# The first stretch of a fused attention and mixture kernel, in an order planned inside the kernel

## The chip, the cores and the metric

The kernel runs on one core of a Trainium2 chip. The metric is the device time of one execution in microseconds. Three runs of the kernel before took 1064.70, 1065.81 and 1065.82 us; the median is 1065.81.

## The reference

Three layers follow each other. The input is 4 batches of 8 heads, 576 tokens and 64 columns a head.

```python
# 1 attention, causal by blocks of 64 tokens
scores = q @ k.T / 8;  scores = where(block_i >= block_j, scores, -1e9)
attn = exp(scores - max) / (sum + 1e-9);  x = attn @ v     # heads side by side: (2304, 512)
# 2 dense unit: maximum of three products, then w_out
h = maximum(maximum(x @ w1, x @ w2), x @ w3)               # 512 -> 768
x = h @ w_out                                              # 768 -> 512
# 3 eight experts (512 -> 1024 -> 512), two per token
noisy = x @ w_gate + log1p(exp(x @ w_noise)) * noise       # the top two, softmax over them
out = sum over the two: weight * (maximum(x @ w1[e], 0) @ w2[e])
```

The weights of the dense layer arrive as 64-bit floats, all else in 32 bits.

## The kernel before

**Attention in jobs.** A job is two heads (a pair) of one batch. Early jobs cover the first 256 tokens of a batch in plain fp32, late jobs the other 320 with each operand split into a high and a low half and three products in place of one. `JOBS` lists them: four early jobs of batch 0, four of batch 1 (jobs 0 to 7), then `MIDDLE`, late and early jobs mixed. Jobs 0 to 7 share four sets of buffers (`SETS`), three of which lie in the tiles that late jobs use afterwards, so that late work can begin only when those jobs are through. An early job has these steps: scores on TensorE (`s_early`, L268), maxima and their scaling on DVE (L275, L277), exponentials on ACT (L280), sums and reciprocals on DVE (L285, L286), scaling of the exponentials on ACT (L294), six turns by TensorE with copies by DVE (`t_early`, L326, L327), and the products with the values (`pv_early`, L360, L361), whose result goes to SBUF as input of a dense unit (L365 for batch 0).

**Dense units.** Nine units of 256 tokens pass layer 2. Unit u < 8 belongs to batch u // 2, even units to early jobs. Unit 0 is computed in plain fp32 from the widened weights (`hidden0`, L519; `columns0`, L541), as the weights are not yet split then; all others with split weights (`hidden`, L561 to L563). The chain `fill` yields them step by step, and `filler(budget)` draws steps of a given cost into the gaps between the steps of the jobs. `CH` is their order, and a unit may be drawn only when its jobs are through (`ready`).

**Weights.** The 64-bit weights come in 24 pieces of 512 KB (18 of the three matrices, six of `w_out`) through 12 staging places. `widen` makes fp32 of a piece: two integer steps on DVE (L438, L439), the low bits on ACT (L440), an integer addition on GpSimd (POOL, L444), and then the load of the piece 12 further on (L432). The gate weights are multiplied into `w_out` (`load_gates`: 24 turns, L456, and 48 small products, L464), so that the columns of unit 0 come in a product of 512 and one of 16. `part` splits the weights into halves (ACT L500, POOL L501): six parts a matrix, then `w_out`. The halves take the places of staging tiles and of widened matrices, and so wait for the additions or products that read those.

**What sets the order.** The program emits steps with generators: `weights(n)` draws n steps of widening, gates or splitting in each gap, `WS` of them, and `warm` issues products of ones (L87), whose results are not used, to keep TensorE busy: 14 ahead of the jobs and three in each gap of jobs 0 to 3. `need(flag)` draws weight steps until a stage is done. All is then ordered by the framework's scheduler, which takes for each engine the ready instruction that was emitted first, by times of its own. Each engine's queue, and SP's queue of loads, runs in the order that results.

Of the kernel before, what the change touches and what calls it, by code (L numbers as in the profile page):

```python
# [36 lines left out]
CH = (0, 2, 4, 1, 6, 3, 5, 7)  # L37
# [15 lines left out]
PER = (0.0, 2.0, 1.0, 1.2)  # L53
WS = (2, 4)
WARM = 3
# [9 lines left out]
def tile_attention_moe_moe(ctx, tc, qT, kT, v, w1, w2, w3, w_out, gates, noise, e1, e2, out):  # L65
# [201 lines left out]
    def s_early(j, c, blocks):  # L267
        st = new_stats(j)  # L268
        q, k, _, p, _ = SET[SETS[j] if j < 8 else 0]
        ps = bank("s")  # L270
        o = (0, 256)
        for x, i in zip(o, blocks):
            nc.tensor.matmul(ps[:, x:x + 64 * i + 64], q[:, i], k[:, :64 * i + 64], start=True, stop=True)
        for a, (x, i) in enumerate(zip(o, blocks)):
            nc.vector.tensor_reduce(st[:, 0, c + a:c + a + 1], ps[:, x:x + 64 * i + 64], axis=AX.X, op=OP.max,  # L275
                                    negate=True)
        nc.vector.tensor_scalar(st[:, 0, c:c + 2], st[:, 0, c:c + 2], 0.125, None, op0=OP.mult)  # L277
        for a, (x, i) in enumerate(zip(o, blocks)):
            n = 64 * i + 64
            nc.scalar.activation(p[:, POFF[i]:POFF[i] + n], ps[:, x:x + n], AF.Exp, bias=st[:, 0, c + a:c + a + 1],  # L280
                                 scale=0.125, accum_out=st[:, 1, c + a:c + a + 1])

    def scale(j, c0, blocks):
        st = ST[j][:, 1, c0:c0 + len(blocks)]
        nc.vector.tensor_scalar(st, st, 1.0e-9, None, op0=OP.add)  # L285
        nc.vector.reciprocal(st, st)  # L286
        for c, i in enumerate(blocks):
            s = ST[j][:, 1, c0 + c:c0 + c + 1]
            if i > 3:
                P = PL[i][:, :64 * i + 64]  # L290
                nc.vector.tensor_scalar(P, P, s, None, op0=OP.mult)
            else:
                P = SET[SETS[j] if j < 8 else 0][3][:, POFF[i]:POFF[i] + 64 * i + 64]
                nc.scalar.activation(P, P, AF.Copy, scale=s)  # L294

# [23 lines left out]
    def t_early(j, key):  # L319
        p, pt = SET[SETS[j] if j < 8 else 0][3:]  # L320
        ps = bank("t")
        blocks = range(4) if key == 0 else (2, 3)
        n = len(blocks)
        for a, i in enumerate(blocks):
            o = POFF[i] + 128 * key
            nc.tensor.transpose(ps[:, 128 * a:128 * a + 128], p[:, o:o + 128], ident)  # L326
        nc.vector.tensor_copy(pt[:, :, 256 * key:256 * key + 64 * n].rearrange("p h (i c) -> p h i c", c=64),  # L327
                              ps[:, :128 * n].rearrange("p (i h c) -> p h i c", i=n, h=2))
# [4 lines left out]
    def new_x(u, g):  # L333
        if u == 8:
            while "u0" not in given:
                next(fill)
            need("so")
            return keep.tile([128, 2, D], F32R, name="xs")
# [13 lines left out]
    EP = {}  # L352

    def pv_early(j, r):
        late, b, g = JOBS[j]
        V, _, pt = SET[SETS[j] if j < 8 else 0][2:]
        if r == 0:
            EP[j] = bank("t")[:, :256]
        p, m = EP[j], slice(64 * r, 64 * r + 64)
        nc.tensor.matmul(p[m], V[:, r, 0:64], pt[:, r, 0:256], start=True, stop=False)  # L360
        nc.tensor.matmul(p[m, 128:256], V[:, r, 64:128], pt[:, r, 256:384], start=False, stop=True)  # L361
        if r:
            x = new_x(2 * b, g)
            if b == 0:
                nc.scalar.activation(x, p, AF.Copy)  # L365
            else:
                nc.scalar.activation(x[:, 0], p, AF.Copy)
                nc.vector.tensor_sub(x[:, 1], p, plain(x[:, 0]))
# [43 lines left out]
    shifted = psS.tile([128, 2, 512], I32, name="a2")  # L412
# [14 lines left out]
    def load_piece(n):  # L427
        if n >= 24:
            return
        src, dst = piece(n)  # L430
# [3 lines left out]
    def widen(n):  # L434
        r, t = stage[n % NW // 3][:, n % 3], shifted[:, n % 2]
        dst = piece(n)[1].bitcast(I32)
        hi, lo = r[:, :, 1], r[:, :, 0]
        nc.vector.tensor_scalar(t, hi, 3, 0x3FFFFFFF, op0=OP.logical_shift_left, op1=OP.bitwise_and)  # L438
        nc.vector.scalar_tensor_tensor(hi, hi, -0x40000000, t, op0=OP.bitwise_and, op1=OP.bitwise_or)  # L439
        nc.scalar.activation(lo, r.bitcast(U16).rearrange("p c (t h) -> p c t h", h=2)[:, :, 0, 1], AF.Copy,  # L440
                             scale=2.0 ** -13)
# [3 lines left out]
        load_piece(n + NW)  # L445

    def load_gates():
        gt = PL[5][:, 128:192].rearrange("p (k n) -> p k n", k=4)
        nc.sync.dma_start(gt, gates.rearrange("(k p) n -> p k n", p=128))
        for g in range(3):  # L450
            wt = []
            for c in range(2):
                ps = bank()
                for k in range(4):
                    o = 256 * c + 128 * (k // 2)
                    nc.tensor.transpose(ps[:, 128 * k:128 * k + 128], WPO[2 * g + k % 2][:, o:o + 128], ident)  # L456
                t = PL[7 + c][:, :512]
                nc.scalar.activation(t, ps, AF.Copy)
                wt += [t[:, 0:256], t[:, 256:512]]
                yield  # L460
            ps = bank()
            for j in range(2):
                for k in range(4):
                    nc.tensor.matmul(ps[:, 2 * E * j:2 * E * j + 2 * E], wt[k][:, 128 * j:128 * j + 128], gt[:, k],  # L464
                                     start=k == 0, stop=k == 3)
            nc.vector.tensor_copy(WPG[:, 2 * g:2 * g + 2], ps[:, :4 * E].rearrange("p (f n) -> p f n", f=2))
            yield

    given = set()

    def convert():
        for n in range(24):
            widen(n)
            if n % 6 == 5:
                given.add(n // 6)
            yield
        for _ in load_gates():
            yield
        given.add("g")

    conversion = convert()
    todo = []

    def weights(n):
        for _ in range(n):
            if next(conversion, 0) == 0 and todo:
                todo.pop(0)()
# [7 lines left out]
    def part(n, i, j, src, flag=None):  # L495
        def do():
            while "g" not in given:
                weights(1)
            wh, wl = (w[:, i, j] for w in halves(n))
            nc.scalar.activation(wh, src, AF.Copy)  # L500
            nc.gpsimd.tensor_sub(wl, src, plain(wh))  # L501
            if flag is not None:
                given.add(flag)
        todo.append(do)

    def need(flag):
        while flag not in given:
            weights(1)

    def hidden0(parts):  # L510
        for fp in range(3):
            need(fp)
            m = None
            for n in ("1", "2", "3"):
                ps = bank().rearrange("p (a b) -> p a b", a=2)
                for j in range(2):
                    f = (2 * fp + j) * 128
                    for kt in range(4):
                        nc.tensor.matmul(ps[:, j], WP[n][:, kt, f:f + 128], XT[0, kt],  # L519
                                         start=kt == 0, stop=kt == 3)  # L520
                if m is None:
                    m = moe.tile([128, 2, UT], F32, name="hh", bufs=3)
                    nc.scalar.activation(m, ps, AF.Copy)
                else:
                    nc.vector.tensor_max(m, ps, m)
                yield 3.3
            parts.append(m)
        for n in ("1", "2", "3"):
            for fp in range(3):
                for k in (0, 2):  # L530
                    s = slice(k, k + 2), slice(256 * fp, 256 * fp + 256)
                    part(n, *s, WP[n][:, s[0], s[1]], ("s", n, fp) if k else None)

    def columns0(parts, tt, x2, gl):
        for w, n in ((WPO, DM), (None, 2 * E)):
            if w is None:
                need("g")
                w = [WPG[:, ft] for ft in range(6)]
            ps = bank()
            for ft in range(6):  # L540
                nc.tensor.matmul(ps[:, :n], parts[ft // 2][:, ft % 2, tt * 128:tt * 128 + 128], w[ft],  # L541
                                 start=ft == 0, stop=ft == 5)
            if n == DM:
                nc.scalar.activation(x2, ps, AF.Copy)
            else:
                nc.vector.tensor_copy(gl[:, tt], ps[:, :n])
            yield n / 100.0

    def hidden(u, parts):
        steps = 0  # L550
        for fp in range(3):
            m = None
            for n in ("1", "2", "3"):
                need(("s", n, fp))
# [46 lines left out]
    def moe1(u):  # L601
        parts = []
        yield from hidden(u, parts) if u else hidden0(parts)
        done.add(u)
        yield 0.01
        need("so" if u else 3)
# [602 lines left out]
```

## Time and profile before

| | |
|---|---|
| Profiled execution | 1064.64 us, span 1062.8 us |
| Mean granted TensorE clock | 0.972 of full speed |
| TensorE busy | 1011.0 us, 95% |
| DVE, ACT, POOL busy | 489.6, 420.2, 457.2 us |
| Moved by DMA | 107.31 MB, mean 101 GB/s |

TensorE is abbreviated PE. Starts and stretches are counted from the start of the span. Matmuls overlap, so that the sum of their durations is more than the time that they take; the spacing of their starts tells that. An fp32 product counts as two matmuls in the rows. The page's chain of waits ends after one step in this case and is of no use; waits and timeline take its place.

### The profile page before, as it was taken

How to read it: one execution, taken by the hardware profiler on the slowest of the kernel's cores; microseconds unless marked ns; L12 is line 12 of the kernel's file. 1: busy time of each engine (PE TensorE's matmuls, PEld its weight loads, DVE VectorE, ACT ScalarE, POOL GpSimd, SP SyncE). 2: the span in 40 equal slices, each digit the busy share in tenths (PEclk: the TensorE clock that was granted, in tenths of full speed). 3: DMA queues.
4: the chain of work that ended last, by engine and by line, in shares of the span. 5: the costliest groups of instructions: out<-in, count | busy, mean ns of one | idle time of the engine just before them, and what ended most of it. 6: DMA issues, size and time to landing. Idle time of an engine off the chain costs nothing. (4 is left out here: it accounts for less than half of the span.)

```text
span 1062.8 us, 17401 instructions
## 1 busy us (share of the span) xinstructions
PE 1011.0 (95%) x6591; PEld 909.2 (86%) x6591; DVE 489.6 (46%) x1324; ACT 420.2 (40%) x1001; POOL 457.2 (43%) x381
## 2 busy tenths in 40 slices
PE   8379999999999999899899899999999999999997
PEld 4257778999999999899899888879898988989895
DVE  6932267596668883885525432122222213222221
ACT  5652344565545662665312333324132323232110
POOL 4750334133232423232314358776564747565302
PEclk9678999999999999999899999999999999999999
DMA  9911032241112120211301256554353534443101
GB/s 292 272 67 26 12 129 73 80 131 41 49 34 70 48 71 16 70 48 46 95 21 51 62 161 219 162 182 155 118 182 93 179 117 131 148 137 120 55 14 64
DMA packets 76263, 107.31 MB, mean 101 GB/s; under 512 B 23672, under 2 KB 48248, under 8 KB 76176
## 3 DMA queue, kind: packets, MB, share of 16 engines
q1 hardware_dynamic: 65584, 76.76, 23.8%
q0 software_dynamic: 10592, 29.41, 8.5%
q8 instruction: 53, 0.87, 0.3%
q14 instruction: 34, 0.28, 0.1%
HBM read 86.66 MB, written 20.53 MB: 101 GB/s over the span
## 5 line engine op out<-in xcount | busy, mean ns | idle before, releaser
L129 POOL TENSOR_TENSOR w<-rw,w 128x1536 fp32r<-128x1536 f32 (+1 forms) x45 | 141.2, 3140 | 76.0 <-ACT w L128 64.3
L128 ACT ACTIVATE w<-rw 128x1536 fp32r<-128x1536 f32 (+1 forms) x45 | 60.4, 1343 | 108.8 <-DMA rw<-in_e 56.7
L939 PE MATMUL b<-xh,w 128*128 128x384 f32 (+7 forms) x272 | 87.0, 321 | 0.9 <-ACT xh L929 0.9
L940 PE MATMUL b<-xl,w 128*128 128x384 f32 (+7 forms) x272 | 87.2, 320 | 0.1
L941 PE MATMUL b<-xh,w 128*128 128x384 f32 (+7 forms) x272 | 87.1, 320 | 0.0
L561 PE MATMUL t<-xA,w 128*128 128x256 f32 x288 | 82.4, 286 | 1.1 <-DVE hm L568 0.9
L562 PE MATMUL t<-xB,w 128*128 128x256 f32 x288 | 82.4, 287 | 0.0
L561 PE MATMUL t<-xB,w 128*128 128x256 f32 x288 | 82.3, 287 | 0.0
L563 PE MATMUL t<-xB,w 128*128 128x256 f32 x288 | 82.0, 285 | 0.0
L562 PE MATMUL t<-xA,w 128*128 128x256 f32 x288 | 81.8, 284 | 0.0
L563 PE MATMUL t<-xA,w 128*128 128x256 f32 x288 | 81.5, 283 | 0.0
L988 POOL DMA_INDIRECT out_rows<-y,isc x40 | 40.5, 1012 | 79.7 <-DVE y L987 72.7
L576 POOL TENSOR_TENSOR hl<-hm,hh 128x512 fp32r<-128x512 f32 x21 | 27.3, 1299 | 107.7 <-ACT hh L575 88.7
L944 DVE SCALAR_TENSOR_TENSOR ht<-b,ht 128x384 fp32r<-128x384 f32 (+6 forms) x56 | 29.1, 520 | 95.8 <-ACT ht L943 95.8
L220 POOL TENSOR_TENSOR Kl<-rk,Kh 128x576 fp32r<-128x576 f32 x16 | 23.7, 1479 | 114.7 <-ACT Kh L219 72.1
L983 PE MATMUL b<-w,ht 128*128 128x512 f32 (+1 forms) x168 | 67.3, 401 | 3.6 <-ACT ht L943 3.6
L941 PE MATMUL t<-xh,w 128*128 128x256 f32 x240 | 67.4, 281 | 0.0
L940 PE MATMUL t<-xl,w 128*128 128x256 f32 x240 | 67.4, 281 | 0.0
L939 PE MATMUL t<-xh,w 128*128 128x256 f32 x240 | 67.0, 281 | 0.0
L985 PE MATMUL b<-w,ht 128*128 128x512 f32 (+1 forms) x168 | 66.7, 397 | 0.0
L984 PE MATMUL b<-w,ht 128*128 128x512 f32 (+1 forms) x168 | 66.5, 396 | 0.0
L987 DVE SCALAR_TENSOR_TENSOR y<-b,idt,prev 128x512 f32<-128x512 f32 (+1 forms) x24 | 18.0, 751 | 104.9 <-PE b L985 91.5
(372 smaller groups left out, 3065.9 us busy)
## 6 DMA issues: line engine op xcount, KB each, us to landing
rw<-in_e SPq DMA_DIRECT2D x32, 768.0 KB, 4.7
w<-in_w SPq DMA_DIRECT2D x18, 512.0 KB, 7.7
rw<-in_e SPq DMA_DIRECT2D x16, 512.0 KB, 3.8
rv<-in_v SPq DMA_DIRECT2D x16, 320.0 KB, 3.0
rk<-in_kT SPq DMA_DIRECT2D x16, 288.0 KB, 2.9
x2d<-x SPq DMA_DIRECT2D x18, 256.0 KB, 2.0
out_rows<-x SPq DMA_DIRECT2D x9, 512.0 KB, 3.9
w<-in_w_out SPq DMA_DIRECT2D x6, 512.0 KB, 5.5
```

What stands on the lines that cost most here:

```text
L128: nc.scalar.activation(t[:, 0, :c], r[:, :c], AF.Copy)
L129: nc.gpsimd.tensor_sub(t[:, 1, :c], r[:, :c], plain(t[:, 0, :c]))
L561: nc.tensor.matmul(ps[:, j], wh, x[:, 0], start=kt == 0, stop=False)
L562: nc.tensor.matmul(ps[:, j], wh, x[:, 1], start=False, stop=False)
L563: nc.tensor.matmul(ps[:, j], wl, x[:, 0], start=False, stop=kt == 3)
L939: nc.tensor.matmul(p, wt1(e, 0, kt, f), th[:, kt, c0:c1], start=kt == 0, stop=False)
L940: nc.tensor.matmul(p, wt1(e, 0, kt, f), tl[:, kt, c0:c1], start=False, stop=False)
L941: nc.tensor.matmul(p, wt1(e, 1, kt, f), th[:, kt, c0:c1], start=False, stop=kt == 3)
L983: nc.tensor.matmul(ps, a, wt2(e, 0, f), start=f == 0, stop=False)
L984: nc.tensor.matmul(ps, a, wt2(e, 1, f), start=False, stop=False)
L985: nc.tensor.matmul(ps, l, wt2(e, 0, f), start=False, stop=f == 7)
L988: st = nc.gpsimd.indirect_dma_start(out=out, out_offset=bass.IndirectOffsetOnAxis(ap=isc[:n, e, c:c + 1], axis=0), in_=y, in_offset=None, ...
```

## The change

The first stretch, which is jobs 0 to 7, the 24 widenings, the gates, the whole of unit 0 and the splitting of all dense weights, is described as 300 steps with an engine, a price in microseconds, what each waits for, and a priority. `Plan.run` goes through time and gives each free engine its ready step of lowest priority. The steps are emitted in order of planned start, inside `tc.manual_schedule()`, within which each engine keeps the order of emission; where instructions emitted outside fall among them stays the scheduler's. While TensorE is free in the plan and the first hidden product has not been placed, it gets one warming product at a time. The unit is no longer in `CH`; the loop over jobs begins at job 8. Within the steps some work changes its engine: the scaling of an early pair's exponentials in this stretch goes from ACT to DVE (jobs 1 and 3) or POOL (the others), the copies of the turns from DVE to ACT, and scores of jobs 1 and 3 use PSUM banks of the other pool.

```diff
-CH = (0, 2, 4, 1, 6, 3, 5, 7)
+CH = (2, 4, 1, 6, 3, 5, 7)
-PER = (0.0, 2.0, 1.0, 1.2)
-WS = (2, 4)
-WARM = 3
+PER = (1.0, 1.2)
+class Plan:
...
+    def run(self, idle=None, until=None):
...
+                ready = [i for i in wait if self.ops[i][0] == e and all(done.get(d, 1e9) <= t for d in self.ops[i][3])
+                         and (self.ops[i][5] is None or self.banks[self.ops[i][5]] > 0)]
+                if not ready:
+                    if e == "PE" and idle and until in wait:
+                        c, f = idle(t)
+                        out.append((t, f))
+                        free[e] = t + c
...
+                i = min(ready, key=lambda i: (self.ops[i][4], i))
...
+        for _, emit in out:
+            emit()
+    def e_scale(j, on):
+        for i, c in EC.items():
...
+            if on != "ACT":
+                (nc.vector if on == "DVE" else nc.gpsimd).tensor_scalar(P, P, x, None, op0=OP.mult)
+            else:
+                nc.scalar.activation(P, P, AF.Copy, scale=x)
...
-    def widen(n):
-        r, t = stage[n % NW // 3][:, n % 3], shifted[:, n % 2]
+    def integers(n):
+        r, t = stage[n % NW // 3][:, n % 3], shifted
...
-        load_piece(n + NW)
+    def start():
+        pl = Plan({"s": 2, "t": 4})
...
+        def idle(t):
+            warmed[0] += 1
+            return 0.43 if t < 7.0 else 0.22, lambda: warm(spare_bank, 1)
...
+        def conv(n, prio):
+            LD[n] = add("SP", 1.38, lambda: load_piece(n), [AD[n - NW]] if n >= NW else [0] if n > 1 else [],
+                        prio, late=2.0)
+        def work(n, prio):
+            a = add("DVE", 1.37, lambda: integers(n), [LD[n]], prio)
+            b = add("ACT", 0.6, lambda: low_bits(n), [LD[n]], prio)
+            AD[n] = add("POOL", 1.05, lambda: join(n), [a, b], prio)
+        def loads(j):
+            old = next((x for x in range(j) if SETS[x] == SETS[j]), None)
+            p = (0.5 if old is None else 30.0) + 0.1 * j
+            LQ[j] = add("SP", 1.1, lambda: load_scores(j), [] if old is None else [ES[old, 1]], p, late=2.0)
+            LV[j] = add("SP", 0.4, lambda: load_rest(j), [LQ[j]] if old is None else [EV[old]], p + (4 if old is None else 0),
+                        late=2.0)
+        def job(j):
+            p = j + 0.5 if j < 4 else 25.0 + j
...
+            r = add("DVE", 0.2, lambda: e_sums(j), ex, p)
+            sc = "DVE" if j in (1, 3) else "POOL"
+            c = add(sc, 1.2 if sc == "DVE" else 1.6, lambda: e_scale(j, sc), [r], p)
...
+            v = add("PE", 0.66, lambda: e_values(j, 0), cp + [LV[j]], p, take="t")
+            v = EV[j] = add("PE", 0.66, lambda: e_values(j, 1), [v], p)
+            EX[j] = add("ACT", 0.35 if j < 4 else 0.8, lambda: e_out(j), [v], p, give="t")
...
+        for n in range(6):
+            conv(n, 0.75 + n if n < 2 else 2.0 + n)
...
+        for n in range(6):
+            work(n, 1.0 + 0.7 * n)
+        for n in range(6, 12):
+            conv(n, 20.0 + n)
+            work(n, 10.0 + n)
...
+        for n in range(12, 24):
+            conv(n, 40.0 + n)
+            work(n, 10.0 + n)
...
+                d = [AD[6 * fp + 2 * m], AD[6 * fp + 2 * m + 1]] + [EX[j] for j in range(4)]
+                a = add("PE", 1.73, lambda fp=fp, m=m: first_hidden(fp, m, 0), d + hid[-1:], 100.0, take="t")
...
+        sp[2] = matrix(2, [AD[n] for n in range(24)] + mats[0] + sp[0] + sp[1][:1])
...
+        so = [part(None, "o", f, slice(0, DM), WPO[f], mats[1] + mats[2] + sp[1] + sp[2], 55.0, 1.26) for f in range(6)]
...
+            a = add("PE", 5.2, lambda tt=tt: first_columns(tt, WPO, DM), [last, prev] + [AD[n] for n in range(18, 24)], 100.0, take="t")
...
-    AHEAD = {-2: [0], -1: [1], **{j: [j + 2] for j in range(6)}, 6: [], **{j: [j + 1] for j in range(7, NJ)}}
+    pl, idle, first_product = start()
+    with tc.manual_schedule():
+        pl.run(idle, first_product)
+    init_route()
+    init_ids()
+    late.append(route(0, C0["g"]))
...
+    load_scores(EJ[0])
+    load_rest(EJ[0])
+    late_tiles()
+    load_job(first)
...
+    for f in score_steps(8):
+        f()
+    scored(8)
+    for j in range(8, NJ):
```

## Rows read from the trace of the kernel before

**Rows 1.** Busy time by stretch: engine busy us (x instructions), granted clock, DMA share, GB/s.
```profile
0.00:30.00 30.00, 24.95 (x107) 14.37 (x107) 19.80 (x71) 18.03 (x52) 12.30 (x31) 0.94 0.94 302
30.00:60.00 30.00, 12.28 (x47) 9.41 (x44) 26.57 (x55) 21.16 (x59) 22.80 (x22) 0.60 0.87 247
60.00:90.00 30.00, 24.83 (x114) 17.36 (x115) 5.47 (x19) 14.48 (x42) 9.66 (x8) 0.72 0.08 19
90.00:150.00 60.00, 60.00 (x288) 44.48 (x287) 21.13 (x48) 17.79 (x47) 19.65 (x17) 1.00 0.10 29
150.00:1062.00 912.00, 888.97 (x6043) 823.59 (x6041) 416.58 (x1134) 348.74 (x805) 392.80 (x304) 0.99 0.31 97
```
The columns of engines are PE, PE's weight loads, DVE, ACT, POOL.

**Rows 2.** Groups of PE's work, 0 to 90 us: busy us, mean ns, idle before.
```profile
L87 PE MATMUL t<-ones 128*128 128x512 bf16 x73 | 23.9, 471 | 1.1 <-DVE cum L656 1.1
```

**Rows 3.** PE's waits, 0 to 90 us: us in total, times, longest.
```profile
PE s L273 <- DMA Kh<-in_kT: 10.6, 1, 10.6
PE t L464 <- ACT p L458: 6.0, 2, 3.7
```

**Rows 4.** Timeline around 90 us: start, us, engine, line, count.
```profile
89.80 0.38 ACT L365 ACTIVATE hl<-t 128x256 f32<-128x256 f32 x1 [3.64 <-PE t L361]
...
90.35 1.36 PE L273 MATMUL s<-kve,qe 128*128 128x256 f32 x8
91.55 0.82 PE L326 MATMUL t<-ident,Ph 128*128 128x128 f32 x6
92.20 7.07 PE L519 MATMUL t<-hl,w 128*128 128x256 f32 x32
99.21 0.66 PE L360 MATMUL t<-Ph,Kh 128*64 128x256 f32 x4
...
100.01 3.72 PE L519 MATMUL t<-hl,w 128*128 128x256 f32 x16
```

**Rows 5.** Timeline of PE, columns of unit 0.
```profile
133.49 3.70 PE L541 MATMUL t<-xB,hh 128*128 128x512 f32 x8
137.03 0.60 PE L326 MATMUL t<-ident,pe 128*128 128x128 f32 x4
...
152.87 1.41 PE L541 MATMUL t<-xs,hh 128*128 128x16 f32 x12
154.13 0.36 PE L561 MATMUL t<-xA,w 128*128 128x256 f32 x1
```

**Rows 6.** SP's loads and the fifth widening in the timeline; landing of the pieces (L432).
```profile
0.75 1.43 SPq L196 DMA_DIRECT2D qe<-in_qT  x2
2.22 0.60 SPq L198 DMA_DIRECT2D kve<-in_kT  x1
2.87 0.43 SPq L432 DMA_DIRECT2D w<-in_w  x1
...
13.21 5.08 SPq L432 DMA_DIRECT2D w<-in_w  x7
...
20.59 0.68 DVE L439 SCALAR_TENSOR_TENSOR w<-w,a 128x512 int32<-128x512 int32 x1
...
DMA to landing us min/median/max: 4.1/6.5/11.1
```

**Rows 7.** Widening and splitting: group on DVE, then lines on POOL (ns min/median/max).
```profile
L438 DVE TENSOR_SCALAR a<-w 128x512 int32<-128x512 int32 x24 | 16.7, 697 | 7.1 <-DMA w<-in_w 6.7
...
L444 POOL TENSOR_TENSOR w<-w x18: 1037/1038/1047, 8.8 to 52.5; 128x512 int32<-128x512 int32 x18
...
L501 POOL TENSOR_TENSOR w<-w x18: 1261/1273/1285, 43.5 to 129.5; 128x512 fp32r<-128x512 f32 x18
```

**Rows 8.** Small steps: maxima's scaling, a fill of 640 columns, a scaling of 320.
```profile
L277 DVE TENSOR_SCALAR st<-st x32: 105/161/1384, 12.4 to 303.9; 128x2 f32<-128x2 f32 x32
...
L178 POOL MEMSET Qh<- x1: 640/640/640, 51.9 to 51.9; 128x640 f32 x1
...
L291 DVE TENSOR_SCALAR p<-p,st 128x320 f32<-128x320 f32 x16 | 6.5, 403 | 0.3
```

More of the change, by code (lines that the diff above doesn't have):

```diff
@@ L469, in tile_attention_moe_moe, with gate_turn @@
[L469 to L487, printed above, removed]
+    GT = PL[5][:, 128:192].rearrange("p (k n) -> p k n", k=4)
+    GS = {}
+    def gate_turn(g, c):
+        ps = GS[g, c] = bank()
+        for k in range(4):
+            o = 256 * c + 128 * (k // 2)
+            nc.tensor.transpose(ps[:, 128 * k:128 * k + 128], WPO[2 * g + k % 2][:, o:o + 128], ident)
@@ L493, in halves @@
         return WH[n], WL[n]
[L495 to L499, printed above, removed]
-            nc.scalar.activation(wh, src, AF.Copy)
[L501 to L510, printed above, removed]
-        for fp in range(3):
[L512 to L528, printed above, removed]
@@ new lines, in split, with first_hidden @@
+    def split(n, i, j, src, low):
+        wh, wl = (w[:, i, j] for w in halves(n))
+        if low:
+            nc.gpsimd.tensor_sub(wl, src, plain(wh))
+        else:
+            nc.scalar.activation(wh, src, AF.Copy)
+    H0 = []
+    def first_hidden(fp, m, j):
+        if j == 0:
+            H0.append(bank().rearrange("p (a b) -> p a b", a=2))
+        f = (2 * fp + j) * 128
+        for kt in range(4):
+            nc.tensor.matmul(H0[-1][:, j], WP[MATS[m][0]][:, kt, f:f + 128], XT[0, kt], start=kt == 0, stop=kt == 3)
@@ new lines, in tile_attention_moe_moe, with first_max, first_columns @@
+    M0 = []
+    def first_max(fp, m):
+        ps = H0[3 * fp + m]
+        if m == 0:
+            M0.append(moe.tile([128, 2, UT], F32, name="hh", bufs=3))
+            nc.scalar.activation(M0[fp], ps, AF.Copy)
+        else:
+            nc.vector.tensor_max(M0[fp], ps, M0[fp])
+    C0 = {}
+    def first_columns(tt, w, n):
+        ps = C0["p"] = bank()
+        for ft in range(6):
+            nc.tensor.matmul(ps[:, :n], M0[ft // 2][:, ft % 2, tt * 128:tt * 128 + 128], w[ft], start=ft == 0,
+                             stop=ft == 5)
@@ L529, in hidden0 @@
             for fp in range(3):
                 for k in (0, 2):
[L531 to L547, printed above, removed]
+                    r.append(part(None, n, slice(k, k + 2), slice(256 * fp, 256 * fp + 256),
+                                  WP[n][:, k:k + 2, 256 * fp:256 * fp + 256], deps + [AD[6 * fp + 2 * m + k // 2]],
+                                  50.0 + m, 1.26))
@@ new lines, in matrix @@
+            return r
+        sp[0] = matrix(0, [AD[n] for n in (0, 1, 2, 12, 13, 14)])
+        sp[1] = matrix(1, [AD[n] for n in (3, 4, 5, 15, 16, 17, 6, 7, 8, 18, 19, 20)] + sp[0][:1])
+        sp[2] = matrix(2, [AD[n] for n in range(24)] + mats[0] + sp[0] + sp[1][:1])
+        done_g = None
+        go = []
+        for g in range(3):
+            cs = []
+            for c in (0, 1):
+                a = add("PE", 0.5, lambda g=g, c=c: gate_turn(g, c), [AD[18 + 2 * g], AD[19 + 2 * g]] + cs, 60.0, take="t")
+                cs.append(add("ACT", 0.65, lambda g=g, c=c: gate_copy(g, c), [a] + ([done_g] if done_g else []), 45.0,
+                              give="t"))
+            done_g = add("PE", 1.7, lambda g=g: gate_product(g), cs + [gt], 60.0, take="t")
+            go.append(add("DVE", 0.2, lambda g=g: gate_out(g), [done_g], 24.0, give="t"))
+            done_g = go[-1]
@@ L549, in hidden @@
+        return pl, idle, hid[0]
     def hidden(u, parts):
@@ L602, in moe1 @@
         parts = []
-        yield from hidden(u, parts) if u else hidden0(parts)
+        yield from hidden(u, parts)
         done.add(u)
         yield 0.01
-        need("so" if u else 3)
         gl = logits()
@@ L609, in moe1 @@
             x2 = keep.tile([128, DM], F32, name="x2", bufs=2)
-            if u == 0:
-                yield from columns0(parts, tt, x2, gl)
-            for c in (0, 264) if u else ():
+            for c in (0, 264):
                 columns(parts, tt, c, 264, x2, gl)
@@ L615, in moe1 @@
             store(u, tt, x2)
-        if not u:
-            for f in range(6):
-                part("o", f, slice(0, DM), WPO[f])
-            part("o", slice(0, 6), slice(DM, NG), WPG, "so")
-            given.add("u0")
         late.append(route(u, gl))
@@ L786, in gap @@
     def gap(j):
[L787 to L792 removed]
+        filler(PER[j >= 16])
     LJ = [j for j in range(NJ) if LATE[j]]
```

295 lines of the change are left out of this document (183 added, 112 removed).

## The prediction

> **What bounds the kernel now.** I read the busy times by stretch first, then TensorE's groups of work and its waits in the first 90 us, then the order of work around 90 and 140 us. In [rows 1] the reader should see two kernels. From 90 us to the end TensorE (PE) is busy 60.0 of 60.0 us and 888.97 of 912 us at a granted clock of 1.00 and 0.99: it is the bound, and little is to be had there. Before 90 us it is not. From 30 to 60 us it is busy 12.28 of 30 us at a clock of 0.60, that is, largely at the lower of its two levels, 1.2 GHz, and from 60 to 90 us at 0.72. Even that busy time is partly idle work: 73 warming products hold 23.9 us [rows 2]. The waits in [rows 3] say why: one wait of 10.6 us for the keys of a second round of pairs, then 6.0 us in two waits for gate copies. DVE, by contrast, is busy 26.57 of 30 us from 30 to 60.
>
> What the first 90 us withhold is the plain dense unit. It can begin only when pair 3 is through, and its output lands at 89.80; the first hidden product of the unit starts at 92.20 [rows 4], although DVE, which widens the weights, is down to 5.47 of 30 us after 60. So the change is worth what it takes out of the time until PE runs without gaps, and no more: PE work is the same before and after, except for the warming.
>
> **Part 1: the work itself, at full clock.** By the starts in [rows 4]: scores of a pair 90.35 to 91.55, 1.2 us; its turns 0.65; 32 hidden products 7.01, so 144 take 31.5; the values of a pair, both halves together, 99.21 to 100.01, 0.8. From [rows 5]: eight column products of 512 take 3.54, so 24 take 10.6, and twelve of 16 columns 1.26, so 24 take 2.5; columns together 13.1. The gates hold 48 products like those of 16 columns, 5.0, and 24 turns of which six are 0.65, 2.6; together 7.6.
>
> **Part 2: where the kernel before stands.** At 90 us all first scores and gates are done, and left of the stretch are four turns (2.6), four values (3.2), hidden products (31.5) and columns (13.1): 50.4 us. PE is dense from there, so the stretch is worth 90 + 50.4 = 140.4 us. (Values with their halves apart cost up to 2.7 more; that goes to the range.)
>
> **Part 3: when the dense unit can start after.** SP issues the loads of four pairs first, each about 2.1 us (0.75 to 2.82 in [rows 6]), so the first weight piece is issued near 7.4 us instead of 2.87, but the sixth near 13.7, much as before (seven pieces go out from 13.21). Landing takes 4.1 to 11.1 us, so the fifth piece lands about when it did: the second half of its widening, begun at 20.59, ended at 21.27. By the priorities in the planner (pair j at j + 0.5, piece n at 1 + 0.7n) DVE's scaling of pair 3 stands just behind that widening. Its chain then is: scaling 1.2 (640 columns in four instructions; 320 take 0.40 [rows 8]), turns 0.65, two copies on ACT of 512 and 256 columns about 1.1 (256 take 0.38 at 89.80 [rows 4]), values 0.8, output 0.38: 21.3 + 4.1 = 25.4, so 26. The bounds: 23, if pieces land two to three microseconds sooner; 31, if each of four handoffs is a POOL instruction late (below).
>
> The small DVE steps on this chain are a cost the planner books at a fixed price. In [rows 8] the scaling of the maxima has a median of 161 ns and a maximum of 1384, and 24 widenings kept POOL in instructions of 1038 ns beside it [rows 7]. I take the median; four waits of a whole POOL instruction, up to 1.27, would be 5 us, which is the bound of 31. The Trainium skill ("SBUF — State Buffer", Who interferes with whom) says that VectorE's two-port modes and GpSimd share one pair of ports as an exclusive lock, and the later one stands still for the whole of the other's instruction; the maximum of 1384 agrees. By that rule alone, three locked steps at 1.27 would put the start at 30, and the time 4 us later than mine; it speaks against moving six pairs' scaling to POOL.
>
> The scaling on POOL has no row. Its bounds for 640 columns are 0.64 (a fill of 640 [rows 8]) and 1.6 (1273 ns for 512 with two inputs [rows 7] in proportion); I take the upper. Pair 2 uses it while pair 3 waits for its piece, so it moves no end.
>
> **Part 4: from there on.** PE then has 31.5 + four pairs of 2.65 (10.6) + gates 7.6 + columns 13.1 = 62.8 us: 26 + 62.8 = 88.8. Nothing else must be later. DMA: its share falls from 0.87 to 0.08 at 60 us [rows 1], so 24 pieces are in by then, and the third part of the unit, due near 26 + 21 + 10, needs only 18 of them. DVE: 24 widenings of two steps at 0.69 [rows 7] are 33 of the 51.8 us that it was busy by 90 [rows 1], and eight pairs of copies leave it for ACT, two pairs' scaling comes. ACT loses the scaling of eight pairs and gains their copies; it was busy 18.03 and 21.16 of 30 us in the first two stretches of [rows 1] and is not near its end. POOL: 24 additions at 1.04, 24 splits at 1.27 and 0.4, six scalings at 1.6: 65.5, and the splits of the third matrix and of the output weights (15.6) wait for hidden products near the end.
>
> Three costs come on top. Every engine keeps the planned order, so where a planned price is short, PE stands: bounds 0 and 20, nearest rows the two waits of 6.0 us together in [rows 3], which the planner's order is there to separate; I take 8, so the stretch ends at 96.8. Second, unit 0 is spent and no longer fills gaps beside the late pairs: the filler's budget is 7, 7, 4, 7, 7 units over pairs 8 to 12 while unit 2 holds 31.5, so it lasts to the end of pair 12 and pair 13 has 7 empty gaps until unit 4 is ready; before, unit 0's remainder covered that. Bounds 0 and 8; I take 4. Third, late pairs begin cold (their buffers are those of pairs 4 to 7): 0 to 5, I take 2; unit 2 and pair 8 stand ready to cover it. The warming products after the plan's first hidden product are gone, but a dense fp32 stream held the clock at 1.00 from 90 us on.
>
> **Sum.** 140.4 - 96.8 = 43.6 won, 6 lost: 37.6. The profiled execution is 1064.64 (span 1062.8 and 1.84 around it), so 1027.0; the median of the runs is 1065.81, 1.17 above, so I state 1028.
>
> **Rivals.**
> *The planned queues block.* In-order engines pass each delay on, and the start of the plan assumes 1.1 us for loads that take 2.1. For it: [rows 1], 30 to 60 us, where the order of before left PE idle 17.7 of 30 us, 10.6 of them in one such wait [rows 3]. Against it: PE has dense products that need no pair at that time. If pairs 4 to 7 cost PE another 30 us at that pace, 17.7 are lost: 1045. Chance 0.16.
>
> *POOL becomes the bound.* It gets 4 to 10 us more work, and unit 2 needs all splits of the three matrices. From 9 us at the pace of 30 to 60 (22.80 of 30, 0.76) its 65.5 take 86 and end at 95, just in time. At 0.55 they end at 128, and PE, with some 10 us of other work, loses 21: 1048. Chance 0.06.
>
> *The cover is missed (slower).* Of the 64 us after 90, 50.4 were this stretch's work, and pairs 8 to 10 ran their long chains beneath it. If those chains need just that cover, all of unit 0's 44.6 us comes back as idle PE beside pairs 8 to 14: 1072. It decides from 37.6 us of idle time on. Against it stands that seven units remain, unit 2 is complete at once, and only pair 13 has no filler by the budgets. Chance 0.05.
>
> *Nothing changes.* The scheduler may still place later work among the planned instructions, and could push them back to the old pace; 1064. Chance 0.03: the order of each engine within the region is fixed.
>
> My forecast has 0.70, with a range of its own from 1010 to 1040. The whole range: start at 23, no stalls, nothing lost and halves that were apart is 20 us below; start at 31, stalls 20 and 13 lost is 24 above. On 1028 that gives 1008 to 1052, which holds the first two rivals too. Two measurements of this kernel can be told apart from about 0.2%, 2 us. Faster: 0.70 + 0.16 + 0.06 and a little of the fourth, 0.93; within, 0.02; slower, 0.05.
>
> **What would show it.** Output of pair 3 between 23 and 31 us, the first hidden product right after; PE busy above 85% from there to about 97; the last gate logits of unit 0 near 97 instead of 154 [rows 5]; no warming after the first hidden product; PE idle time of a few us near pair 13; POOL's last split before 100. The forecast is wrong if the first hidden product starts after 35, if PE idles over 20 us between it and the last column, or if idle time after 150 us rises far above the 23 us of [rows 1].

## The result, and the profile after

The kernel after takes 1041.01 us (median; 1033.54 to 1042.27) against 1065.82 for the kernel before beside it: a ratio of 0.9755, with an interval of 0.9715 to 0.9796. That is faster by 24.8 us; 37.8 were forecast. The profiled execution took 1033.54 us, the shortest of the runs, 31.1 below that of before. The others are 6 to 9 us longer, at a mean clock of 0.980 to 0.985 against 0.987; no trace shows where.

Busy time by stretch after, columns as in [rows 1]:

```profile
0.00:30.00 30.00, 20.07 (x108) 12.34 (x108) 19.74 (x68) 14.19 (x47) 14.41 (x35) 1.00 0.79 223
30.00:60.00 30.00, 26.93 (x133) 21.84 (x134) 22.55 (x42) 19.46 (x45) 18.54 (x20) 0.94 0.97 318
60.00:90.00 30.00, 25.74 (x147) 21.34 (x146) 20.12 (x47) 20.03 (x61) 27.64 (x30) 0.89 0.18 52
90.00:150.00 60.00, 59.29 (x396) 50.54 (x395) 33.45 (x104) 28.42 (x80) 29.78 (x28) 1.00 0.22 68
150.00:1031.00 881.00, 855.70 (x5780) 791.49 (x5778) 400.25 (x1058) 332.69 (x756) 382.77 (x294) 0.99 0.31 97
180.00:200.00 20.00, 17.54 (x137) 16.35 (x137) 17.86 (x71) 11.77 (x35) 3.06 (x5) 1.00 0.34 109
```

Against [rows 1], PE is up from 12.28 to 26.93 us in the second stretch and its clock from 0.60 to 0.94. After 150 us it is busy for 33.3 us less and idle for 25.3 us in place of 23.0. The difference, 31.0, is that of the spans.

What leads to the unit on DVE and ACT, then PE up to the last column (timeline after; start, duration). L445 on ACT copies the output of a pair, here pairs 2 and 3; L522 at 25.67 is the fifth widening's second step, L358 pair 3's scaling, L406 the copies of the turns of pairs 2 and 3, and L526 the low bits of a piece:

```profile
25.67 0.69 DVE L522 SCALAR_TENSOR_TENSOR w<-w,a 128x512 int32<-128x512 int32 x1
...
26.80 1.71 DVE L358 TENSOR_SCALAR Pl<-Pl,st 128x256 f32<-128x256 f32 x4
...
29.29 0.71 ACT L526 ACTIVATE w<-w 128x512 int32<-128x512 uint16 x1 [3.22 <-DMA w<-in_w]
29.89 1.60 ACT L406 ACTIVATE Pl<-t 128x512 f32<-128x512 f32 x4
...
32.17 0.36 ACT L445 ACTIVATE hl<-t 128x256 f32<-128x256 f32 x1
32.90 0.69 ACT L526 ACTIVATE w<-w 128x512 int32<-128x512 uint16 x1 [0.37 <-DMA w<-in_w]
34.37 0.67 ACT L526 ACTIVATE w<-w 128x512 int32<-128x512 uint16 x1 [0.79 <-DMA w<-in_w]
34.93 0.37 ACT L445 ACTIVATE hl<-t 128x256 f32<-128x256 f32 x1
```

```profile
35.41 0.59 PE L136 MATMUL a<-ones 128*128 128x512 bf16 x1 [1.51 <-DVE w L522]
35.79 3.30 PE L580 MATMUL t<-hl,w 128*128 128x256 f32 x8
38.93 1.36 PE L327 MATMUL s<-Kh,Qh 128*128 128x256 f32 x8
40.13 3.62 PE L580 MATMUL t<-hl,w 128*128 128x256 f32 x16
...
115.00 1.41 PE L597 MATMUL t<-xs,hh 128*128 128x16 f32 x12
```

The output of pair 3 is the second of the two copies and ends at 35.30. Ahead of it in ACT's planned order stand low bits of pieces that have not landed yet; ACT waits 3.22, 0.37 and 0.79 us for them. The first hidden product starts at 35.79, where 26 was forecast and [rows 4] has 92.20. The first eight take 3.30 us and the next sixteen 3.62: from 36 to 39 us the granted clock was 0.56, near the lower of its two levels. The last columns end at 116.41, where [rows 5] has 154.28. In between PE is idle for 4.6 us (columns as in [rows 1]):

```profile
35.80:116.40 80.60, 75.97 (x390) 60.82 (x389) 53.20 (x109) 48.09 (x124) 63.14 (x63) 0.94 0.39 128
```

What PE waited for, 0 to 120 us, and the warming of the plan, 0 to 117 us (waits; a group):

```profile
PE a L136 <- DVE w L522: 9.8, 7, 2.2
PE t L399 <- POOL Ph L358: 1.5, 3, 1.0
```

```profile
L136 PE MATMUL a<-ones 128*128 128x512 bf16 x40 | 12.1, 433 | 10.8 <-DVE w L522 9.8 <-DVE cum L829 1.1
```

The longest wait is that of the warming: idle work that waits for DVE. Its products write the second half of a PSUM tile, `a2`, whose first half the widening uses, and the rows show the two taking turns.

SP and POOL in the first 27 us (timeline):

```profile
6.74 0.43 SPq L516 DMA_DIRECT2D w<-in_w  x1
...
13.05 2.54 SPq L516 DMA_DIRECT2D w<-in_w  x3
16.62 0.37 SPq L828 DMA_DIRECT2D noise<-in_noise  x1
17.05 5.29 SPq L256 DMA_DIRECT2D rq<-in_qT  x1
...
23.72 0.47 SPq L516 DMA_DIRECT2D w<-in_w  x1
```

```profile
9.64 2.66 POOL L358 TENSOR_SCALAR pe<-pe,st 128x256 f32<-128x256 f32 x4 [4.57 <-ACT Ph L340]
...
24.11 2.65 POOL L358 TENSOR_SCALAR Ph<-Ph,st 128x256 f32<-128x256 f32 x4
```

The first piece goes out at 6.74 (7.4 forecast). Then the framework's scheduler puts loads of the first late job among the planned ones, one of which holds SP for 5.29 us (0.34 is that line's median in this trace). The scaling of a pair costs POOL 2.66 us, over the bound of 1.6.

### The profile page after: what moved, and what is told of

The parts are those of the page before. It is cut to its first block, busy times and chain, and to the rows that moved or that the text cites. A ratio compares the mean times of both kernels' runs of the same rounds, so it can differ in the third digit from the quotient of the medians.

```text
span 1031.8 us, 17326 instructions
## 1 busy us (share of the span) xinstructions
PE 987.7 (96%) x6557; PEld 897.5 (87%) x6557; DVE 496.1 (48%) x1316; ACT 414.8 (40%) x985; POOL 473.2 (46%) x405
```

## The experiments

Twelve kernels ran. The table has the median, the ratio's interval, and from the profiled execution its time, the start of the first hidden product and the end of the last columns of unit 0.

| kernel | median us | ratio, 95% | profiled | first hidden | columns end |
|---|---|---|---|---|---|
| before | 1065.8 | | 1064.6 | 92.2 | 154.3 |
| after | 1041.0 | .9715-.9796 | 1033.5 | 35.8 | 116.4 |
| e1_own_bank | 1036.1 | .9696-.9742 | 1036.1 | 34.7 | 118.0 |
| e2_no_warm | 1031.2 | .9658-.9688 | 1031.2 | 31.8 | 112.4 |
| e3_free_order | 1041.1 | .9754-.9792 | 1039.5 | 28.2 | 121.9 |
| e4_old_engines | 1035.5 | .9704-.9736 | 1033.1 | 43.3 | 117.7 |
| b1_before_no_warm | 1057.1 | .9891-.9921 | 1059.6 | 85.2 | 150.1 |
| e5_late_loads | 1043.2 | .9725-.9787 | 1044.1 | 35.8 | 125.3 |
| e6_nowarm_loads | 1029.9 | .9625-.9666 | 1039.1 | 30.7 | 122.5 |
| e7_prices | 1036.1 | .9681-.9732 | 1036.1 | 24.8 | 118.4 |
| e9_no_small | 1028.9 | .9632-.9679 | 1028.9 | 24.4 | 113.5 |
| e10_no_small | 1025.1 | .9582-.9630 | 1027.4 | 29.5 | 110.2 |
| e12_low_on_pool | 1026.9 | .9598-.9639 | 1028.4 | 24.3 | 108.6 |
| e13_pool_price | 1035.0 | .9679-.9715 | 1035.0 | 28.3 | 119.8 |

The last column tells the time: profiled time less columns' end is 915 to 920 us in all kernels with the plan, and 910 in the two without. The start of the first hidden product does not: 24.8 and 43.3 go with nearly the same median.

**e1: warming in a PSUM bank of its own.**

```diff
-    both = psS.tile([128, 2, 512], I32, name="a2")
-    shifted, spare_bank = both[:, 0], both[:, 1].bitcast(F32)
+    shifted = psS.tile([128, 2, 512], I32, name="a2")[:, 0]
+    spare_bank = bank("t")
-        pl = Plan({"s": 2, "t": 4})
+        pl = Plan({"s": 2, "t": 3})
```

> The warming products get a PSUM bank of their own instead of the second half of the tile whose first half the widening writes (the plan counts one bank less for all else until the first hidden product). Theory A, the shared tile: TensorE's warming waits for DVE's second widening step (9.8 us in 7 waits) and DVE's first step waits for the warming (4.2 us in 5), though the data are apart; without that the first hidden product moves from 35.8 to 25 to 30 us and the time falls by 6 to 10 us below the changed kernel's median of 1041, to about 1033. Rival B, the loads: the pieces and values land no sooner, the waits only change their name to DMA waits; first hidden product at 34 to 37 and the time within 3 us of 1041.

1036.07, first hidden product at 34.7. PE's waits, 0 to 120 us:

```profile
PE t L399 <- POOL Ph L358: 3.7, 5, 2.0
PE t L399 <- ACT Pl L406: 3.6, 1, 3.6
```

The waits of the warming for the widening are gone, so the shared tile made them. The start hardly moves, as rival B has it: waits for POOL's scaling and for ACT's copies of the turns take their place. The edit also takes a bank from the rest of the plan, so it is no pure test. The time is 4.9 us below after, between the theories; the intervals of the two ratios overlap, and the columns of the profiled execution end later (118.0 for 116.4).

**e2: no warming in the plan.**

```diff
-        pl.run(idle, first_product)
+        pl.run(None, first_product)
```

> No warming products in the plan at all. Theory A: the waits on the shared tile are gone as well, first hidden product at 25 to 30 us; the clock before it is at the lower level for some of the pairs' products, which costs 1 to 3 us; time about 1034. Rival C, warming is worth its cost: the clock falls until the dense unit and the time is 1041 or more.

1031.2: 9.8 us less than after, a little more than theory A had; the start is 31.8 and not 25 to 30. The clock is lower in the first 30 us (0.86 for 1.00), and the time is shorter all the same. The traces show only part of the 9.8, as that of after is its shortest execution: the columns end 4.0 us earlier. PE's waits now show what the warming had covered (8.8 us in all for POOL's scaling):

```profile
PE t L399 <- POOL Ph L358: 8.8, 4, 8.1
PE s L327 <- DMA kve<-in_kT: 4.8, 1, 4.8
```

**e3: the planned steps without the fixed region.**

```diff
-    with tc.manual_schedule():
-        pl.run(idle, first_product)
+    pl.run(idle, first_product)
```

> The same 300 steps in the same order of emission and on the same engines, but without the region that fixes each engine's order: the scheduler orders them. Theory D, the fixed order carries the gain: the scheduler hoists weight and gate work past the pairs as before, first hidden product after 45 us, time 1050 or more. Rival E, the emission order already carries it: first hidden product within 4 us of 35.8 and the time within 5 us of 1041.

1041.09: no difference from after. The order in which the steps are emitted carries the gain, the fixed region adds nothing that can be measured. Rival E has the time right, though not the start: the dense unit starts 7.6 us earlier, and PE gives it back in one wait, at which a late job's scores need the tile of the widening:

```profile
PE a L290 <- DVE w L522: 10.9, 1, 10.9
```

**e4: scaling back on ACT, copies back on DVE, the plan kept.**

```diff
-            c = add(sc, 1.2 if sc == "DVE" else 1.6, lambda: e_scale(j, sc), [r], p)
+            c = add("ACT", 1.4, lambda: e_scale(j, "ACT"), [r], p)
-                cp.append(add("ACT", (0.55, 0.4)[key], lambda key=key: e_copy(j, key, "ACT"),
+                cp.append(add("DVE", (0.68, 0.42)[key], lambda key=key: e_copy(j, key, "DVE"),
```

> The plan as it is, but the scaling of the exponentials of pairs 0 to 7 on ACT and the copies of their turns on DVE, as in the kernel before (priced 1.4, and 0.68 and 0.42). Theory D, the order carries the gain: time within 5 us of 1041, first hidden product 33 to 39 us. Rival F, moving this work between engines carries it: the time is 1052 or more, half way back.

1035.52, no longer than after: moving scaling to POOL and copies to ACT is no part of the gain, against rival F. The first hidden product is the latest of all, 43.3, where theory D had 33 to 39, and its columns end 1.3 us after those of after: PE had done other work of the plan first.

**b1: the kernel before without warming.**

```diff
-WM = (14, 0, 0, 0, 0)
+WM = (0, 0, 0, 0, 0)
-WARM = 3
+WARM = 0
```

> The kernel before, without its warming products (none ahead of the jobs, none in the gaps); nothing of the change. Theory A, the change wins by starting the plain dense unit at 36 instead of 92 us: warming was not what held the unit, so this stays within 4 us of 1066. Rival B, the change wins because 33 of the 74 warming products are gone from TensorE's queue (23.9 us busy): 1046 or less.

1057.08, between the two theories: warming costs the old kernel 9.6 us. So the plan is worth 24.8 us with warming in both and 25.9 without (1057.08 - 1031.2): the two effects add.

**e5 and e6: noise and the first late job's loads made steps of the plan behind the widening of piece 12, with warming (e5) and without (e6).**

```diff
+        for f in (lambda: nc.sync.dma_start(noise_sb, noise.rearrange("(t p) e -> p t e", p=128)),
+                  lambda: load_job(first), lambda: load_values(first)):
+            add("SP", 0.7, f, [AD[12]], 90.0)
-    load_job(first)
-    load_values(first)
```

> The changed kernel with its warming; only the noise and the three loads of the first late job, which the scheduler hoists between the planned loads at 16.6 us, are made steps of the plan behind the widening of piece 12. Theory A, hoisted loads block SP's queue for 6.6 us (one issue of 5.3 us), piece 6 is late, ACT stands in order before pair 3's copies: first hidden product at 29 to 33 us instead of 35.8, time 1034 to 1038. Rival B, pieces are limited by bandwidth and the waits on the shared PSUM tile set the start: 34 or later, and within 3 us of 1041.

1043.19, first hidden product again at 35.8. This is rival B: while warming and widening share a tile, SP's blocked queue doesn't set the start. PE's waits (the second is for a long DVE step, 9.15 us, of the kind that e9 shows):

```profile
PE a L136 <- DVE w L522: 10.4, 7, 2.1
PE a L291 <- DVE Ql L275: 4.4, 1, 4.4
```

> The same with no warming products. Theory A: both causes are gone, first hidden product at 26 to 29 us (31.8 without warming alone), time 1025 to 1029. Rival B: the loads are not on the path once warming is gone: 31 to 32 us and 1031, as without warming alone.

1029.89 (1026.92 to 1039.07), not to be told apart from e2: the loads give nothing measurable. The profiled execution is its longest; DVE spends 7.01 us there on one tiny step (4 elements a partition), in a stretch in which POOL never pauses. e9 and e10 test whether the two belong together.

**e7: e6 with three prices of the plan corrected.**

```diff
-            LQ[j] = add("SP", 1.1, lambda: load_scores(j), [] if old is None else [ES[old, 1]], p, late=2.0)
+            LQ[j] = add("SP", 2.05, lambda: load_scores(j), [] if old is None else [ES[old, 1]], p, late=2.0)
-                        prio, late=2.0)
+                        prio, late=4.3)
-            c = add(sc, 1.2 if sc == "DVE" else 1.6, lambda: e_scale(j, sc), [r], p)
+            c = add(sc, 1.2 if sc == "DVE" else 2.66, lambda: e_scale(j, sc), [r], p)
```

> As the run before, and three prices of the plan are set to what the trace shows: 2.05 instead of 1.1 for the loads of a pair, 4.3 instead of 2.0 from a piece's issue to its landing, 2.66 instead of 1.6 for a pair's scaling on POOL. Theory A, a plan that knows the late landing no longer queues pair 2's second maximum and pair 3's steps behind pieces that are not there: first hidden product at 23 to 26 us, time 1022 to 1026. Rival B, landing varies so much that prices change little: within 2 us of the run before.

The start is 24.8, within the forecast's 23 to 31 and as theory A has it, yet the time is 1036.07 and not 1022 to 1026: 6.2 longer than e6, so that rival B missed too. Three prices changed at once; e13 shows what POOL's alone does. DVE, POOL and PE from 72 to 88 us (timeline):

```profile
72.81 13.96 DVE L334 TENSOR_SCALAR st<-st 128x2 f32<-128x2 f32 x1
86.68 0.41 DVE L332 TENSOR_REDUCE st<-s 128x1 f32<-128x64 f32 x2
...
74.05 11.06 POOL L569 TENSOR_TENSOR w<-w 128x512 fp32r<-128x512 f32 x9
85.06 1.69 POOL L284 TENSOR_TENSOR V<-rv,V 128x320 fp32r<-128x320 f32 x2
...
87.44 0.69 PE L399 MATMUL t<-ident,pe 128*128 128x128 f32 x2 [10.31 <-DVE xs L558]
```

A DVE step on two numbers a partition, with a median of 169 ns, lasts 13.96 us and ends at 86.77, as POOL's run of eleven instructions ends at 86.75. PE stands for 10.3 us behind it. The time lies inside the step's row and not in a wait ahead of it: it looks as if the step had begun and did not get through. e9 tests that.

**e9 and e10: e7 and e6 with the two tiny DVE steps of the early pairs gone.**

```diff
-        nc.vector.tensor_scalar(st[:, 0, 2 * h:2 * h + 2], st[:, 0, 2 * h:2 * h + 2], 0.125, None, op0=OP.mult)
+        nc.scalar.activation(st[:, 0, 2 * h:2 * h + 2], st[:, 0, 2 * h:2 * h + 2], AF.Copy, scale=0.125)
-        nc.vector.tensor_scalar(st, st, 1.0e-9, None, op0=OP.add)
```

(The second line is in front of the exps, the third in `e_sums`.)

> The kernel of e7_prices (no warming, late loads planned, prices corrected; first hidden product at 24.8, then PE idle 10.3 us before 87.4 because one DVE TENSOR_SCALAR of 128x2 elements lasted 13.96 us, from 72.81 to 86.77, while POOL ran TENSOR_TENSOR steps back to back until 86.75). Changed: the two tiny DVE TENSOR_SCALAR steps of the early pairs are gone; the factor 0.125 on the two negated maxima is taken by ACT in front of the exps, the added 1e-9 on the four sums is left out. Theory A (that DVE form, both operands in SBUF, cannot get in while POOL runs back to back): no DVE step of the early pairs lasts over 1.2 us, the 10 us gap at 77 to 87 is gone, last gate products some 8 to 10 us earlier, time 1024 to 1030. Theory B (the order of the plan makes DVE and PE stand there, the long row is only where the wait is shown): another DVE row or wait of 8 us or more stands at the same place and the time stays at 1033 to 1039.

1028.93: 7.1 us won over e7 and the gap is gone, as theory A has it. But the next DVE step of such a kind met the same run of POOL (DVE, then POOL; timeline of e9):

```profile
90.41 12.52 DVE L275 SCALAR_TENSOR_TENSOR Ql<-rq,Qh 64x320 fp32r<-64x320 f32 x2 [0.34 <-ACT Qh L274]
...
94.68 6.17 POOL L568 TENSOR_TENSOR w<-xB,w 128x512 fp32r<-128x512 f32 x5
100.79 1.27 POOL L568 TENSOR_TENSOR w<-hl,w 128x512 fp32r<-128x512 f32 x1
```

It ends at 102.93, 0.9 us behind POOL's 102.06; 12.00 of the 12.52 us belong to one of the two steps. But not every step waits for the whole run. In the trace of after the same two steps took 2.92 us, from 100.98, although POOL ran on without a pause from 102.12 to 110.70, and a small step got through in 1.12 us, at the end of one of POOL's seven instructions (timeline of after):

```profile
85.31 1.12 DVE L350 TENSOR_SCALAR st<-st 128x4 f32<-128x4 f32 x1 [2.06 <-ACT pe L340]
...
82.69 8.64 POOL L569 TENSOR_TENSOR w<-w 128x512 fp32r<-128x512 f32 x7
```

What decides whether a step gets through after one instruction or after the run stays open.

> The kernel of e6_nowarm_loads (1029.89; first hidden product at 30.7; a DVE TENSOR_SCALAR of 128x4 lasted 7.01 us from 84.38 to 91.39 while POOL ran back to back until 91.37) with the same two tiny DVE steps of the early pairs gone. Theory A (POOL's back-to-back run keeps that DVE form out): PE's wait of 5.6 us at 90 to 96 shrinks under 2 us, time 1023 to 1028. Theory B (order of the plan): a wait of 4 us or more remains at that place and the time stays at 1028 to 1033.

1025.14, 4.7 below e6 (the intervals just overlap), the fastest of all: 41.4 below the kernel before (1066.53 beside it), and a ratio of 0.9606 where after has 0.9755. As theory A has it, PE never stops at 90 to 120 us. Its longest wait before 120 us is now at another place, 18.6 to 24.4, for POOL's scaling of pair 2. That wait, and PE in its windows:

```profile
24.40 1.91 PE L398 MATMUL t<-ident,Ph 128*128 128x128 f32 x6 [5.79 <-POOL Ph L357]
```

```profile
60.00:90.00 30.00, 25.64 (x154) 21.72 (x155) 13.16 (x29) 22.98 (x70) 28.05 (x28) 0.89 0.21 58
90.00:120.00 30.00, 30.00 (x174) 23.34 (x173) 19.33 (x61) 12.95 (x37) 14.11 (x12) 1.00 0.28 96
```

**e12: e9 with the late queries' low bits on POOL.**

```diff
-            nc.scalar.activation(h, src, AF.Copy, scale=0.125)
-            nc.vector.scalar_tensor_tensor(l, src, 0.125, plain(h), op0=OP.mult, op1=OP.subtract)
+            nc.scalar.activation(src, src, AF.Copy, scale=0.125)
+            nc.scalar.activation(h, src, AF.Copy)
+            nc.gpsimd.tensor_sub(l, src, plain(h))
```

> The kernel of e9_no_small (1028.93; there the pair of DVE SCALAR_TENSOR_TENSOR steps that make the low bits of a late job's queries took 12.52 us, from 90.41 to 102.93, with POOL back to back until 102.06, and PE stood 7.3 us behind it). Changed: these low bits are taken by POOL (tensor_sub of 64x320, twice a job), with the factor 0.125 taken by ACT first. Theory A (DVE steps that read and write SBUF alone are kept out while POOL runs back to back): no DVE step between 60 and 110 lasts over 3 us, PE's wait of 7.3 us on L557 is gone or moves to a wait on POOL itself of 0 to 5 us, since POOL was busy 29.80 of 30 us there; time 1022 to 1028. Theory B (the low bits are late because their inputs are late): PE's wait stays at 7 us or more, time 1028 to 1033.

1026.94. PE's wait of 7.3 us is gone; one of 6.3 stands instead, in which a gate turn waits for POOL's addition of a `w_out` piece, and the columns end 4.9 us earlier. The median is 2.0 below e9, with intervals that overlap. POOL's own load is the longest wait left here.

**e13: e10 with POOL's true price.**

```diff
-            c = add(sc, 1.2 if sc == "DVE" else 1.6, lambda: e_scale(j, sc), [r], p)
+            c = add(sc, 1.2 if sc == "DVE" else 2.66, lambda: e_scale(j, sc), [r], p)
```

> The kernel of e10_no_small (1025.14; first hidden product at 29.5; PE waits 6.3 us in all for POOL's scaling of early pairs) with one price in the plan changed: POOL's scaling of a pair 2.66 us, as measured, instead of 1.6. Theory A (the wrong price makes the plan put pair 3's turn in front of other work that was ready): PE's waits for POOL scaling fall under 3 us, first hidden product 26 to 29, time 1021 to 1025. Theory B (POOL's own duration and not its price is what delays; or a start a few us earlier is given back later): waits for POOL scaling stay over 4 us or another wait takes their place, time 1024 to 1029.

Both theories missed: PE's wait for POOL's scaling fell to 2.8 us and the start came to 28.3 as A says, but the time is 1035.03, 9.9 worse than e10. The new order puts the low bits of a late job under POOL's long run, and PE waits 5.1 us for them (timeline, DVE then POOL; then PE's wait). From 90 to 120 us the granted clock is 0.77, where e10 has 1.00; how the 9.9 us divide between wait and clock is not shown.

```profile
89.99 13.51 DVE L275 SCALAR_TENSOR_TENSOR Ql<-rq,Qh 64x320 fp32r<-64x320 f32 x2 [0.53 <-ACT Qh L274]
...
97.71 4.92 POOL L568 TENSOR_TENSOR w<-xB,w 128x512 fp32r<-128x512 f32 x4
```

```profile
PE a L291 <- DVE Ql L275: 5.1, 1, 5.1
```

Of the profiled executions, e5, e6, e7, e9 and e13 have a DVE step of 7 us or more before 160 us; before, b1, e2, e4, e10 and e12 have none that is 1.3 us over its median.

## Why the prediction held, and where its size was off

The measured time lies in the whole range of 1008 to 1052, which was drawn to hold two rivals too. The forecast itself had a narrower one, 1010 to 1040, and the median is 1.0 us above it. By the first of its own signs, a first hidden product after 35 us, the forecast fails as well, by 0.8 us; the other two do not show (PE idles 4.6 us of the allowed 20 up to the last column, and 25.3 us for 23 after 150 us).

**What bounds the kernel (right).** PE was idle for 27.9 of the first 90 us and is for 17.3 after. The columns end 37.9 us earlier (154.3 to 116.4), where 43.6 were forecast (140.4 to 96.8). The count of Part 2 left out 13.9 us. By the spacing of starts some 10 of them are work of later pairs that the scheduler had put into the stretch, among them 24 products of late scores; most of the rest is values with their halves apart, which the prediction had left to the range.

**Part 3, the start at 26 (the mis-sized term).** It came at 35.8, and its bound of 31 was too low too. The first piece was issued as worked out (6.74 for 7.4), and pair 3's scaling does stand just behind the fifth widening. But that widening ends at 26.36, where 21.27 was taken, and the chain from there to the end of pair 3's output, worked out as 4.1, took 8.9 us (35.30). Three things stand in the place of the missing 9.8:

- "PE work is the same before and after, except for the warming" took warming as free before the dense unit. DVE waits for it in the shared tile (2.6 us in three waits before the fifth widening ends), and one more warming product stands right in front of the first hidden product. Without warming the start is 31.8 (e2). In time it cost 9.8 us in the kernel after (e2) and 9.6 in the one before (b1); the shared tile's part of it (4.9 in e1) is not clear of noise.
- "SP issues" missed the scheduler's own loads, 5.3 us in SP's queue; moved away, and without warming, the start is 30.7 (e6).
- The planned order rests on prices that were too low: in the plan a piece lands 3.4 us after its issue begins (1.38 and 2.0), where the trace has 6.7 at the least; the loads of a pair take 2.05 for 1.1, and POOL's scaling 2.66 for 1.6 ("I take the upper": a price from an instruction with two inputs did not bound it). Low bits of pieces that have not landed thus stand in ACT's order in front of pair 3's copies and output, and ACT waits 4.4 us for them. With the three prices raised the start is 24.8 (e7), the largest step of the three; POOL's price alone moved it by 1.2 (e10 to e13), and the other two were not tried apart.

That 24.8 meets the forecast's 26 is luck all the same, since the raised prices changed the order: in e7 pair 3's scaling stands behind the third widening, which ends at 20.14, and no longer behind the fifth (25.23), and the output ends 5.2 us later, at 25.38. In the order that Part 3 assumes, without warming and with the loads moved (e6), the fifth widening ends at 24.12 and the chain behind it takes 7.1 us (4.1 worked out). Both terms were too short, and why the fifth widening is still 2.9 us late there is not shown.

**Part 4, "26 + 62.8" (near in sum, by other terms).** From start to columns it was 80.6 us; 70.8 were forecast, 8 of them stalls. PE idled 4.6. Work of later pairs takes some 7 by the spacing of starts, and the rest, some 69, is the stretch's own 62.8 at a mean clock of 0.94 and with values in halves. The table shows besides that a start moved by 10 us moves the end little: PE did other planned work first (e4), or gave the time back in a stall at 60 to 105 us (e3, e7, e13). The term "stalls 8" hides what decided between the variants.

**The small DVE steps (the wrong bound).** "Four waits of a whole POOL instruction, up to 1.27" supposed that a step waits for one instruction. Some do (1.12 us at 85.31 in after), but a single one can wait for POOL's whole run: 13.96 us (e7), 12.00 (e9) and nearly all of 13.51 (e13). The Trainium skill ("SBUF — State Buffer", Who interferes with whom) says that a GpSimd operation and a VectorE one in a two-port mode, or a GpSimd one that reads SBUF and a VectorE one with two inputs there, exclude each other, and that the later one waits out the other's whole instruction. The traces agree on who is kept out, and in the long cases disagree on how long. In the kernel after itself one such step lasted 3.2 us, at 74.87; no wait names it.

**After the stretch.** The forecast was 6 lost: 37.9 - 31.1 = 6.8 were. The size is in part luck: PE's idle time behind the last column grew by only 3.0 us (23.0 to 26.0), and the rest is busy time, such as later work that the kernel before had done inside the stretch. Near pair 13 PE is idle 2.5 us of 20 (4 forecast; 180 to 200 us above). POOL's last split ended at 110.7, not before 100.

**The sum.** 37.9 - 6.8 = 31.1 in the profiled execution, 37.6 forecast; the median gives 24.8, and what makes the other runs 6 to 9 us longer stays open. e2, without warming, spreads by 2.3 us, but e6, also without, by 12.1.

**The rivals.** *The planned queues block* (1045) is nearer to the median than the forecast (1028), and its mechanism is there, but at pairs 0 to 3 and not at 4 to 7. *POOL the bound* didn't decide in the kernel after; in e12 PE's longest wait is for POOL. *The cover is missed* and *nothing changes* are out.

## What to carry to other kernels

Judge a reordering by when its stretch ends, not by when its main work starts: an earlier start is often given back at the next in-order wait. Drop warming when it shares a buffer, or an engine's order, with work on the path. Where an engine idles behind a long row of a tiny step, look at what its neighbour ran back to back.

## What was unexpected of the hardware

Beside POOL's back-to-back instructions, DVE steps of two forms can stand still for longer than one of them, at times until the whole run ends: TENSOR_SCALAR of fp32 from SBUF to SBUF (13.96 us for 128x2 in e7) and SCALAR_TENSOR_TENSOR with both inputs in SBUF (12.00 us for one of 64x320 in e9). Others of the same forms got in after one instruction (1.12 us for 128x4 in after), and no run shows what decides. e9 took the first of these steps out, and the stall at that place went. In the kernel after, RECIPROCAL of 128x4 stayed at a mean of 180 ns, and 24 widening steps, which have an operand in PSUM, at 696 and 691. And TENSOR_SCALAR of 640 columns took POOL 2.66 us where DVE had needed 1.2 for four steps of its pair 1 (355, 314, 280 and 249 ns).
